# When the halo copy of sliding v and the loads behind it are issued, in an attention kernel overlapped with an MLP

## The chip, the cores and the metric

The kernel runs on one core of a Trainium2 chip. The metric is the device time of one execution, in microseconds (us). 13 runs of the kernel before took 307.81 to 313.6 us, with a median of 309.58 us.

A core has five engines with their own instruction queues: TensorE (PE: matmuls; PEld is its weight load), VectorE (DVE), ScalarE (ACT), GpSimd (POOL) and SyncE (SP). SP computes nothing here; it issues transfers. POOL issues transfers too, in another queue. Each engine executes its own instructions in order, so a wait at the head of a queue holds up all that stands behind it.

## The reference

What is computed, cut down (B, H, S, D = 8, 8, 576, 64; hidden width 2048):

```
scores = scale * q @ k.T                              # per batch row and head
mask_plain = (rel >= 0) & (rel < 32)                  # heads 0 to 3, "sliding"
mask_dil   = (rel >= 0) & (rel < 128) & (rel % 4 == 0)  # heads 4 to 7, "dilated"
attn = softmax(where(mask, scores, -1e9))
x    = (attn @ v).transpose(0, 2, 1, 3).reshape(4608, 512)
out  = relu(x @ w_in) ** 2 @ w_out                    # [512, 2048], [2048, 512]
```

rel is the position of the query less that of the key, so a query sees its last 32 positions, or each fourth of its last 128.

## The kernel before

**Attention.** The work goes by batch row b, 0 to 7. Sliding heads are cut into six blocks of 96 queries; a block's keys are its 96 positions and the 32 before them. So in `vp`, the fp16 tile of sliding v, partitions 32 to 127 hold a block's own values and partitions 0 to 31 the last 32 of the block before it. These 32 are the *halo*. `load_sliding_v` (L125) brings fp32 v into `sv`, `cast_sliding_v` (L167, three casts on POOL) makes `vp` of it, and the halo is copied inside `vp`: by `halo_sliding` (L182, ACT, in three parts) in rows 0 to 2, by `halo_sliding_by_dma` (L193, a transfer from SP) from row 3 on. Dilated v goes the same way: `load_dilated_v` (L134) to `sd`, `cast_dilated_v` (L173, four casts on POOL) to `vd`, and `halo_dilated` (L188) or `halo_dilated_by_dma` (L196).

Queries and keys must lie with the head dimension on partitions, in `QKTp` (sliding) and `QKTd` (dilated). From row 2 on the DMA transposes them. Sliding: POOL loads `ns` (L109), DVE reorders it by token into `nr` (L118), SP writes that to a DRAM tile `dp` (L214) and issues two transposes of it (`transpose_sliding`, L223), keys (i = 1) and then queries (i = 0). Dilated: POOL writes the DRAM tile `dd` (L204), SP issues two transposes of that (L227).

Per row, `attn_scores` (L692) makes the two sliding and two dilated groups of scores; each goes through exp on ACT and a mask multiplication on DVE (L564) into `AT`. The values follow: `av_sliding` (L616) for three pairs of blocks, `av_dilated` (L633) for the rest. Each is normalised on DVE (L605, L610) and turned into `xT`, the input of the MLP. Rows 1 to 3 do that on PE (`attn_values`, L706); rows 4 to 7 turn it by DMA (`attn_values_by_dma`, L737), with the tiles `xs`, `xd` and `yd`.

**The MLP as filler.** Tokens are worked in nine chunks of 512. `moe_gen` (L498) is a generator: 32 steps of the first product (L298; two full-width matmuls a step, relu on ACT L321, square on DVE L322), then the second product (L375, from chunk 2 on by one level of Strassen, with sums `gs` made on DVE at L331, L332 and L418). `pump(n)` takes n steps of it. The attention of row b is written between steps of chunk b - 1, so PE has matmuls while ACT and DVE work on scores; how many steps lie between two pieces of attention is a number in the code.

**The order of transfers** is the written one. While row b is worked, row b + 1 is made ready. In rows 2 and 3 one function does it, `turn_and_load` (L854): nr and dp, the load of sliding v, the load of dilated v, the sliding and the dilated transposes, all on SP, then both casts on POOL. Row 2 calls it after the third sliding product, row 3 after its last scores. From row 4 on it is three functions (L880 to L894): `copied` after the second sliding product, `first` and `second` after the transposes of yd. The halo transfers stand at the head of the next row (L851, L876), behind the stores of the MLP's results that were issued in between.

At the head of a row, POOL runs `after_transposes` (L234): it copies one element of `QKTd` into the tile `seen`, so that POOL waits there until the dilated query transpose has landed, and only then issues the loads of ns and dd for the next row. From row 5 on the cast of the row's dilated v stands behind these.

Two of the buffers of `ns` and `nr`, `QKTp`, `QKTd`, `vp` and `vd` exist, taken in turn; `sv` and `sd` exist once.

Of the kernel before, what the change touches and what calls it, by code (L numbers as in the profile page):

```python
# [17 lines left out]
def kernel(  # L18
# [9 lines left out]
    nc = tc.nc  # L28
# [105 lines left out]
    def load_dilated_v(b, eng):  # L134
        vv = v[b, HH:H].rearrange("h (i c) d -> i h (c d)", c=DIL)
        for t in range(2):
            eng.dma_start(out=sd[P - QD[t] : P, t, :, :], in_=vv[Q0D[t] : Q0D[t] + QD[t]])
# [29 lines left out]
    def cast_sliding_v(b, ms=range(0, NB, 2)):  # L167
        for m in ms:
            nc.gpsimd.tensor_copy(  # L169
                vp[b % 2][:, m : m + 2, :, 0:D], sv[:, :, m : m + 2, :].rearrange("p h m d -> p m h d")  # L170
            )

    def cast_dilated_v(b):  # L173
        for t in range(2):
            p0 = 64 * t
            for c in range(0, DIL, 2):
                nc.gpsimd.tensor_copy(  # L177
                    vd[b % 2][p0:P, t, c : c + 2, :, 0:D],
                    sd[p0:P, t, :, D * c : D * (c + 2)].rearrange("p h (c d) -> p c h d", d=D),
                )  # L180

    def halo_sliding(b, mp):  # L182
        m0, m1 = max(1, 2 * mp), 2 * mp + 2
        nc.scalar.copy(
            vp[b % 2][0:PADP, m0:m1, :, 0:D], vp[b % 2][P - PADP : P, m0 - 1 : m1 - 1, :, 0:D]
        )
# [6 lines left out]
    def halo_sliding_by_dma(b):  # L193
        nc.sync.dma_start(out=vp[b % 2][0:PADP, 1:NB], in_=vp[b % 2][P - PADP : P, 0 : NB - 1])
# [4 lines left out]
    def cast_v(b):  # L199
        cast_sliding_v(b)  # L200
        cast_dilated_v(b)
# [22 lines left out]
        for i in (1, 0):  # L224
            nc.sync.dma_start_transpose(out=QKTp[b % 2][:, i, :, PADP:], in_=dp[i])

    def transpose_dilated(b, dd):  # L227
        for i in (1, 0):
            nc.sync.dma_start_transpose(out=QKTd[b % 2][:, i, :, KPAD:], in_=dd[i])


# [280 lines left out]
    def pump(n):  # L512
        for _ in range(n):
            while pending:
                try:
                    next(pending[0])
                    break
                except StopIteration:
                    pending.pop(0)
# [46 lines left out]
    def s_sliding(b, hp):  # L566
        tiles = [pa(f"ps{b}_{hp}_{half}") for half in range(2)]
        for half, ps in enumerate(tiles):
            for m3 in range(3):
                m = 3 * half + m3  # L570
                for e in range(2):
                    r = slice(D * e, D * (e + 1))
                    nc.tensor.matmul(  # L573
                        ps[:, e, QB * m3 : QB * (m3 + 1)],
                        QKTp[b % 2][r, 1, hp, QB * m : QB * m + P],
                        QKTp[b % 2][r, 0, hp, PADP + QB * m : PADP + QB * (m + 1)],
                        start=True,
                        stop=True,
                    )
        for half, ps in enumerate(tiles):  # L580
            softmax(2 * hp + half, ps, maskp)
# [30 lines left out]
    def x_tiles(b):  # L612
        x = xp.tile([QB, 2, NB, 2, D], FP16, name=f"xs{b}", tag="xs")
        return x, [xp.tile([QD[t], DIL, HH, D], FP16, name=f"xd{b}_{t}", tag=f"xd{t}") for t in range(2)]
# [77 lines left out]
    def attn_scores(b, gap, less=0, hooks={}):  # L692
        for hp in range(2):
            s_sliding(b, hp)
            if hp in hooks:
                hooks[hp]()
            pump(gap)
        for g in range(2):
            s_dilated(b, g)
            if 2 + g in hooks:  # L700
                hooks[2 + g]()
            if g and b < 3:
                halo_sliding(b, 0)
            pump(gap - less)

    def attn_values(b, gap, wide=False, then=None):  # L706
        xs = x_tiles(b)
        for mp in range(3):
            av_sliding(b, mp, xs)
            if b < 3:  # L710
                if mp < 2:
                    halo_sliding(b, mp + 1)
                else:
                    halo_dilated(b, 0)
            if then and b == 2 and mp == 2:
                then()
            pump(gap)
        x_sliding(b, 0, xs, wide)
        if b < 3:
            halo_dilated(b, 2)  # L720
        pump(gap)
        av_dilated(b, 0, 0, xs)
        if then and b == 1:
            then()
        pump(gap)
        x_sliding(b, 1, xs, wide)
        pump(gap)
        av_dilated(b, 0, 1, xs)
        pump(gap)
        for a in range(2):  # L730
            av_dilated(b, 1, a, xs)
            pump(gap)
        x_dilated(b, 0, xs, wide)
        pump(gap)
        x_dilated(b, 1, xs, wide)
# [61 lines left out]
    dd = keep_dilated_qk(2)  # L797
# [28 lines left out]
    for a in range(2):  # L826
        t_dilated(1, m, a, True)
        pump(2)
    attn_scores(1, 2, 1)
    dp = []  # L830
    attn_values(1, 1, True, lambda: dp.append(keep_sliding_qk(2, by_token(2, ns))))
    pump(1000)
# [2 lines left out]
    leave_first()  # L835
    load_v(2)


    def turn(b, n):
        return keep_sliding_qk(b, by_token(b, n))  # L840

    for b in range(2, 4):
        pending.append(moe_gen(b - 1))
        nxt = b + 1
        after_transposes(b)
        ns = load_sliding_qk(nxt)
        if b == 2:
            cast_v(b)
        dd = keep_dilated_qk(nxt)
        if b == 3:  # L850
            halo_sliding_by_dma(b)  # L851
            halo_dilated_by_dma(b)

        def turn_and_load():  # L854
            dp = turn(nxt, ns)
            load_sliding_v(nxt)
            load_dilated_v(nxt, nc.sync)
            transpose_sliding(nxt, dp)
            transpose_dilated(nxt, dd)
            cast_v(nxt)  # L860

        pump(22 if b == 2 else 12)
        attn_scores(b, 4, 0, {3: turn_and_load} if b == 3 else {})
        attn_values(b, b, False, turn_and_load)
        pump(1000)

    for b in range(4, B):
        pending.append(moe_gen(b - 1))
        nxt = b + 1
        if nxt < B:  # L870
            after_transposes(b)
            ns = load_sliding_qk(nxt)
            dd = keep_dilated_qk(nxt)
        if b > 4:
            cast_dilated_v(b)
        halo_sliding_by_dma(b)  # L876
        halo_dilated_by_dma(b)
        dps = []

        def copied():  # L880
            if nxt < B:
                dps.append(turn(nxt, ns))

        def first(y):
            if nxt < B:
                load_sliding_v(nxt)

        def second(y):
            if nxt < B:
                transpose_sliding(nxt, dps[0])  # L890
                transpose_dilated(nxt, dd)
                load_dilated_v(nxt, nc.sync)
                nc.gpsimd.tensor_copy(seen, y[:, 0, 0, 0:1])
                cast_sliding_v(nxt)  # L894

        pump(3)
        attn_scores(b, 3)
        attn_values_by_dma(b, (copied, first, second))
        pump(1000)
# [33 lines left out]
```

## Time and profile before

| | |
|---|---|
| median of 13 runs | 309.58 us (307.81 to 313.6) |
| the profiled execution's own time | 311.42 us |
| its span, first to last instruction | 309.6 us |
| PE busy | 289.0 us, 93% of the span |
| DVE, ACT, POOL busy | 68%, 56%, 21% |
| the DMA queue of SP and ACT | 32.96 MB, 51.1% of 16 engines' span |
| the DMA queue of POOL | 13.63 MB, 25.8% |
| chain that ended last | PE 72%, DMA 12%, DVE 6%, SP's queue 4% |

How to read what follows. A *wait* line names the waiting engine, its line and what it waited for, then the sum in us, how often, and the longest. A *timeline* line has the start and the length in us, the engine, the line, the operation, out<-in with the tiles' names and their shapes, and how often in a row; square brackets hold the idle time before it and what ended it. The *chain of waits* is followed back from the last instruction, at each step to what released it. "Landing" is the time from a transfer's issue to the arrival of its data. The granted clock is TensorE's, as a share of full speed.

Times in the profile count from the span's start. Row 3's scores begin at about 100 us, row 4's at 127.9, row 5's at 157.6, row 6's at 190.4, row 7's at 224.3; from 254 us on only the MLP is left.

### The profile page before, as it was taken

Reading aid. Unit: us, or ns where it says so; the run is one execution under the profiler, and the core shown is the slowest. Engines: PE = TensorE matmul, PEld = TensorE weight load, DVE = VectorE, ACT = ScalarE, POOL = GpSimd, SP = SyncE. Lnnn points to the kernel's source line nnn. Section 1 sums busy time; section 2 is a strip of 40 time slices with the busy share of each in tenths; the row PEclk is TensorE's granted clock in tenths of the full one; section 3 lists DMA queues with packets and bytes.
Section 4 is the critical chain, followed back from the end, with each engine's and each line's share of the span. In section 5 each row is a group of like instructions: output and inputs, shape, how many; then the busy total and the mean of one; then the engine's idle time right before and its main releaser. Section 6 shows DMA issues by size and latency. Waiting matters only on the chain.

```text
span 309.6 us, 6899 instructions
## 1 busy us (share of the span) xinstructions
PE 289.0 (93%) x2762; PEld 193.5 (62%) x2762; DVE 210.8 (68%) x434; ACT 172.9 (56%) x293; POOL 64.7 (21%) x112
## 2 busy tenths in 40 slices
PE   1888998999999999999996999799999999999994
PEld 1555554455554579657886986358845885685584
DVE  7784449668844798499657975879389934834652
ACT  2856638569735942784475545554395436525620
POOL 4473008002806305300224003500240000000000
PEclk9999999999999999999999999989999999999999
DMA  7899997899599999987899789969993231003004
GB/s 116 166 216 213 208 169 135 200 196 224 109 230 190 233 211 161 257 160 138 155 185 261 156 132 199 274 125 140 145 270 26 42 93 62 2 1 135 2 1 139
DMA packets 77617, 47.04 MB, mean 152 GB/s; under 512 B 58480, under 2 KB 69232, under 8 KB 77584
## 3 DMA queue, kind: packets, MB, share of 16 engines
q1 hardware_dynamic: 68832, 32.96, 51.1%
q0 software_dynamic: 8752, 13.63, 25.8%
q8 instruction: 22, 0.36, 0.5%
q14 instruction: 11, 0.09, 0.1%
HBM read 36.70 MB, written 16.52 MB: 172 GB/s over the span
## 4 chain that ended last, share of the span: by engine, by line
PE 72%; DMA 12%; DVE 6%; SPq 4%; ACT 2%; issue 2%; POOL 1%; DVEq 0%; POOLq 0%
PE ph L298 32%; PE pa L375 16%; PE pb L375 7%; DMA vp<-vp 6%; PE po L441 5%; PE pc L375 4%; DVE AT L564 3%; DMA QKTd<-dd 3%; PE paw L638 2%; DMA QKTp<-dp 2%; PE pav L622 2%; DMA ns<-in_q_dram 1%; PE ps L573 1%; PE pf L507 1%; SPq L132 1%
## 5 line engine op out<-in xcount | busy, mean ns | idle before, releaser
L298 PE MATMUL ph<-xT,wi 128*128 128x512 f16 (+1 forms) x640 | 135.7, 361 | 0.7 <-ACT xT L675 0.7
L321 ACT ACTIVATE rt<-ph 128x512 f16<-128x512 f32 x144 | 86.2, 609 | 51.1 <-PE ph L298 49.6
L298 PEld LDWEIGHTS <-wi 128*128 128x128 f16 x640 | 68.4, 114 | 46.8 <-issue 2.0
L322 DVE TENSOR_TENSOR g<-rt 128x512 f16<-128x512 f16 x144 | 63.3, 448 | 40.7 <-ACT rt L321 39.2
L375 PEld LDWEIGHTS <-g 128*128 128x128 f16 x448 | 43.3, 98 | 6.1
L375 PEld LDWEIGHTS <-gs 128*128 128x128 f16 x336 | 32.2, 98 | 3.9 <-DVE gs L332 0.3
L441 PE MATMUL po<-wo,g 128*128 128x512 f16 x128 | 33.1, 379 | 0.0
L402 DVE TENSOR_TENSOR ov<-pb,ov 128x512 f32<-128x512 f32 x14 | 9.7, 692 | 31.1 <-PE pb L375 17.4
L375 PE MATMUL pa<-wt,gs 128*128 128x256 f16 x224 | 27.2, 273 | 0.0
L375 PE MATMUL pb<-wt,g 128*128 128x256 f16 x224 | 27.1, 273 | 0.0
L169 POOL CAST vp<-sv 128x512 f16<-128x512 f32 x24 | 14.8, 648 | 54.2 <-DMA sv<-in_v_dram 47.5
L391 ACT COPY ov<-pa 128x512 f32<-128x512 f32 x14 | 8.2, 586 | 30.7 <-PE pa L375 30.7
L177 POOL CAST vd<-sd 128x512 f16<-128x512 f32 (+1 forms) x32 | 22.6, 732 | 11.6 <-DMA sd<-in_v_dram 11.2
L610 DVE TENSOR_TENSOR xd<-paw,rcp_d 80x512 f16<-80x512 f32 (+1 forms) x32 | 21.9, 684 | 1.1
L563 ACT ACTIVATE AT<-pz 128x576 f16<-128x576 f32 x32 | 19.7, 694 | 1.2 <-PE pz L592 1.1
L564 DVE TENSOR_TENSOR AT<-AT,maskd 128x576 f16<-128x576 f16 x32 | 18.9, 617 | 1.9 <-ACT AT L563 0.8
L563 ACT ACTIVATE AT<-ps 128x576 f16<-128x576 f32 x32 | 19.2, 657 | 1.3 <-PE ps L573 0.8
L564 DVE TENSOR_TENSOR AT<-AT,maskp 128x576 f16<-128x576 f16 x32 | 16.2, 520 | 5.2 <-ACT AT L563 3.5
L622 PEld LDWEIGHTS <-AT 128*128 128x128 f16 x192 | 9.5, 99 | 13.7 <-issue 9.8
L391 ACT COPY ou<-pa 128x512 f32<-128x512 f32 x14 | 8.2, 586 | 17.4 <-PE pa L375 17.4
L622 PE MATMUL pav<-vp,AT 128*128 128x65 f16 x192 | 10.9, 196 | 7.4 <-DMA vp<-vp 5.7
L610 DVE TENSOR_TENSOR xs<-pav,rcp_p 96x512 f16<-96x512 f32 x24 | 16.5, 687 | 0.8
(80 smaller groups left out, 278.3 us busy)
## 6 DMA issues: line engine op xcount, KB each, us to landing
sv<-in_v_dram SPq DMA_DIRECT2D x14, 288.0 KB, 5.3
dp<-nr SPq DMA_DIRECT2D x12, 288.0 KB, 4.2
out_dram<-ou SPq DMA_DIRECT2D x6, 512.0 KB, 4.1
out_dram<-ov SPq DMA_DIRECT2D x6, 512.0 KB, 4.6
sd<-in_v_dram SPq DMA_DIRECT2D x8, 320.0 KB, 6.1
ns<-in_k_dram POOLq DMA_DIRECT2D x8, 288.0 KB, 6.3
ns<-in_q_dram POOLq DMA_DIRECT2D x8, 288.0 KB, 7.7
sd<-in_v_dram SPq DMA_DIRECT2D x8, 256.0 KB, 6.2
```

The lines of the kernel that those rows point to most:

```text
L169: nc.gpsimd.tensor_copy(vp[b % 2][:, m : m + 2, :, 0:D], sv[:, :, m : m + 2, :].rearrange("p h m d -> p m h d"))
L177: nc.gpsimd.tensor_copy(vd[b % 2][p0:P, t, c : c + 2, :, 0:D], sd[p0:P, t, :, D * c : D * (c + 2)].rearrange("p h (c d) -> p c h d", d=D),)
L298: nc.tensor.matmul(ph[:, t0:t1], wi4[ffc // 4][:, dmk, :, ffc % 4], xT[:, dmk, x0 : x0 + t1 - t0], start=(dmk == 0 and t0 == 0), stop=(dmk ...
L321: nc.scalar.activation(rt, ph[:], ACTF.Relu)
L322: nc.vector.tensor_mul(g[:, ffc, :], rt, rt)
L375: nc.tensor.matmul(banks[bank][:, t], a(k, t), b(k), start=(new and t == 0 and k == 0), stop=(k == HF - 1), skip_group_check=True,)
L391: nc.scalar.copy(ot, banks[A])
L441: nc.tensor.matmul(po, g[:, ffc, t * P : (t + 1) * P], wo[ffc // 4][:, ffc % 4, :], start=(ffc == 0), stop=(ffc == NFF - 1),)
L563: nc.scalar.activation(AT[:, u, 0:UW], ps[:, :, 0 : UW // 2], ACTF.Exp, scale=scale)
L564: nc.vector.tensor_mul(AT[:, u, 0:UW], AT[:, u, 0:UW], mask)
L610: nc.vector.tensor_tensor(out=x, in0=pv, in1=rb, op=ALU.mult)
L622: nc.tensor.matmul(pav[:, i, h * (D + 2) : h * (D + 2) + D + 1], AT[:, 2 * (h // 2) + m // 3, off : off + P], vp[b % 2][:, m, h, 0 : D + 1 ...
```

## The change

1. `transpose_dilated` takes the sides that it is to do. A new function does four things in a row: the dilated keys' transpose, the halo transfer of sliding v, the dilated queries' transpose, the load of dilated v. So for rows 3 to 7 the halo's issue leaves the head of the row and stands between the two transposes on SP. It reads what POOL's sliding cast writes, so SP waits there for that cast.
2. In `turn_and_load` (making ready rows 3 and 4) the load of dilated v goes behind all four transposes. The sliding cast stays; the dilated cast goes to the head of the row, on POOL behind `seen` and the loads of ns and dd, where rows 5 to 7 already had it.
3. From row 4 on, the sliding cast is written before the dilated transposes. POOL's own order is the same.
4. Row 2 calls `turn_and_load` after its second sliding product, not its third.
5. Row 3's scores begin after 9 steps of the MLP, not 12.
6. Row 1's first halo copy (ACT) stands after its second group of sliding scores, not after its last dilated scores.

```diff
-    def transpose_dilated(b, dd):
-        for i in (1, 0):
+    def transpose_dilated(b, dd, sides=(1, 0)):
+        for i in sides:
             nc.sync.dma_start_transpose(out=QKTd[b % 2][:, i, :, KPAD:], in_=dd[i])
...
-            if g and b < 3:
+            if g and b == 2:
                 halo_sliding(b, 0)
...
-            if then and b == 2 and mp == 2:
+            if then and b == 2 and mp == 1:
                 then()
...
-    attn_scores(1, 2, 1)
+    attn_scores(1, 2, 1, {1: lambda: halo_sliding(1, 0)})
...
+    def transpose_and_load(b, dd):
+        transpose_dilated(b, dd, (1,))
+        halo_sliding_by_dma(b)
+        transpose_dilated(b, dd, (0,))
+        load_dilated_v(b, nc.sync)
...
         if b == 3:
-            halo_sliding_by_dma(b)
+            cast_dilated_v(b)
             halo_dilated_by_dma(b)
 
         def turn_and_load():
             dp = turn(nxt, ns)
             load_sliding_v(nxt)
-            load_dilated_v(nxt, nc.sync)
             transpose_sliding(nxt, dp)
-            transpose_dilated(nxt, dd)
-            cast_v(nxt)
-
-        pump(22 if b == 2 else 12)
+            cast_sliding_v(nxt)
+            transpose_and_load(nxt, dd)
+
+        pump(22 if b == 2 else 9)
...
-        if b > 4:
-            cast_dilated_v(b)
-        halo_sliding_by_dma(b)
+        cast_dilated_v(b)
         halo_dilated_by_dma(b)
...
         def second(y):
             if nxt < B:
                 transpose_sliding(nxt, dps[0])
-                transpose_dilated(nxt, dd)
-                load_dilated_v(nxt, nc.sync)
                 nc.gpsimd.tensor_copy(seen, y[:, 0, 0, 0:1])
                 cast_sliding_v(nxt)
+                transpose_and_load(nxt, dd)
```

## The prediction

> **What bounds the kernel now.** The first view is the page: PE is busy 93% of the span and its chain is 72% PE, so a saving must be a place where PE waits. The waits of PE name one that this change touches: 5.7 us in three places, for the copy of the sliding v halo (vp<-vp).
>
> ```profile
> PE pav L622 <- DMA vp<-vp: 5.7, 3, 2.7
> ```
>
> Next, busy time by stretch, one stretch from the first scores of a row to the next row's: rows 3, 4, 5, 6, 7. Behind each length stand PE, PEld, DVE, ACT, POOL busy, then PE's clock.
>
> ```profile
> 99.80:127.60 27.80, 27.31 (x299) 19.72 (x298) 21.79 (x44) 15.40 (x28) 6.87 (x13) 1.00 1.12 206
> 127.60:157.40 29.80, 29.80 (x295) 21.34 (x294) 23.03 (x48) 18.03 (x31) 4.46 (x9) 1.00 0.89 169
> 157.40:190.20 32.80, 30.09 (x349) 27.01 (x347) 24.67 (x48) 17.92 (x31) 7.74 (x13) 1.00 0.95 185
> 190.20:224.10 33.90, 31.59 (x290) 21.31 (x288) 24.44 (x48) 17.93 (x31) 7.49 (x13) 0.95 0.91 176
> 224.10:253.70 29.60, 28.94 (x285) 20.36 (x284) 22.79 (x46) 17.88 (x30) 3.14 (x4) 1.00 0.48 100
> ```
>
> Row 4 has no idle PE and takes 29.8 us. Rows 5 and 6 do the same work in 3.0 and 4.1 us more. The chain shows why in row 5: the second dilated transpose lands, GpSimd's one-element read sees it, and only then is the halo issued, behind the v loads and two stores; it needs 7.1 us.
>
> ```profile
> 154.67 0.75 SPq L229
> ...
> 155.51 4.59 DMA QKTd<-dd
> ...
> 160.22 0.35 POOL seen L235
> 160.58 7.11 DMA vp<-vp
> ...
> 167.73 0.29 PE pav L622 x4
> ```
>
> The timeline has the stop in each row, and the DVE copy nr<-ns, which turns the next row's q and k and runs next but one behind it on DVE:
>
> ```profile
> 138.44 0.75 DVE L120 COPY nr<-ns 128x2304 f16<-128x2304 f16 x1
> ...
> 167.73 0.29 PE L622 MATMUL pav<-vp,AT 128*128 128x65 f16 x4 [2.71 <-DMA vp<-vp]
> ...
> 171.17 0.75 DVE L120 COPY nr<-ns 128x2304 f16<-128x2304 f16 x1
> ...
> 200.06 0.33 PE L622 MATMUL pav<-vp,AT 128*128 128x65 f16 x4 [2.31 <-DMA vp<-vp]
> ...
> 200.20 2.75 PE L298 MATMUL ph<-xT,wi 128*128 128x512 f16 x6
> ...
> 204.80 0.74 DVE L120 COPY nr<-ns 128x2304 f16<-128x2304 f16 x1
> ...
> 232.30 0.29 PE L622 MATMUL pav<-vp,AT 128*128 128x65 f16 x4 [0.66 <-DMA vp<-vp]
> ```
>
> In row 6 six matmuls take 2.75 us where row 7 has 1.46: after the 2.31 us stop the granted clock was 0.52 from 200.06 to 203.6, which costs about 1.7 us more. Row 5's 2.71 us stop was not followed by that. [...]
>
> **The halo, rows 5 to 7.** It goes between the two dilated transposes, at 155.5 in row 5. It must wait for GpSimd's sliding cast, which in the old rows ends at 154.44, 187.12 and 220.95, while the first dilated transpose leaves SP at 155.4, 188.5 and 221.7: no wait. It needs 2.8 to 7.5 us to land (the extremes of its five issues), so by 163.0 at the latest in row 5, and PE asks at 165.0. The three stops go.
>
> What is late next? The halo's issue (0.61 to 1.10 us on SP) stands before the second transpose, so that, the dilated v load, both stores, and GpSimd's "seen" read come later. Bounds: 0.2 us, if the transpose queue is what limits SP here (one transpose took 2.39 us to issue in row 5, 1.27 in row 6), to 1.1. I take 0.7, nearest to the 0.61 and 0.68 issues among the quieter queues. Behind "seen" on GpSimd stand the loads of ns and dd and the cast of the dilated v, and ns feeds nr. The landings from issue, rows 5 and 6:
>
> ```profile
> DMA to landing us min/median/max: 7.3/7.7/8.2
> DMA to landing us min/median/max: 8.7/9.1/9.5
> ```
>
> The later ns half is issued at 161.44 and 193.31, so it lands at 169.6 and 202.8. New: +0.7, and -0.3 because 82.5 KB of halo (at the 270 GB/s of the page's fullest slices) no longer lie in front: 170.0 and 203.2. Row 4 shows what an unhindered row wants: nr 3.56 us after the first pav (134.88 to 138.44), that is 168.3 and 201.0. So DVE will wait where PE waited. From nr on, DVE has no gap for 7.8 us in rows 4, 5 and 6 (138.44 to gs L332 at 146.25; 171.17 to 178.99; 204.80 to 212.70), and PE's product from gs starts within 0.7 us of that. The vd halo, 0.7 later as well, lands at about 171.7 in row 5; its reader comes 9.5 us after the first pav (row 4), at 174.2: covered. The row therefore ends earlier by what nr gains: 171.17 - 170.0 = 1.2 in row 5, 204.80 - 203.2 = 1.6 in row 6 (the slow clock's 1.7 us goes, but ns hides most of it). Bounds: 0 (ns 1.6 us later than I say) to 2.9 and 3.8 (nr at 168.3 and 201.0).
>
> Row 7 has no nr, but DVE is busy until 233.2 with masks and squares, and the normalisation starts there: of 0.66 us I take 0.3 (0 to 0.66).
>
> **Rows 3 and 4.** Row 3's turn moves one sliding product earlier: nr at about 82.5 instead of 83.83. The 0.74 us copy now delays the third normalisation; its next reader on PE is over 1 us later: nothing. SP then issues dp and sv, and no longer sd (2.74 us of issue, 89.28 to 92.0) before the sliding transposes. They landed at 100.05, and PE waited 0.2 us for them; new about 97. The pump of 12 becomes 9, so scores begin three steps of 0.435 us earlier, 98.5 instead of 99.8: covered by 1.5 us; no matmul is added or dropped. Gain 0.2. The halo now waits on SP for the cast (sv lands about 93.8, three casts of 0.62: 95.8), and behind it are the second dilated transpose (landing about 100.3, wanted at 102.9), sd, three stores and the vd halo (wanted after 115). In row 4 it waits alike, to about 120.7, and the transpose lands near 125, wanted at 131. Each is covered.
>
> The dilated cast is what pays. It ran at 97.1 to 100.1 and 121.6 to 124.0, ahead of the scores. New: it follows "seen" and four load issues (0.56 to 0.66 us each) and waits for sd; I put it at 104.5 to 107.5 and 128.2 to 131.3, beside the scores. There DVE slows:
>
> ```profile
> L564 DVE TENSOR_TENSOR AT<-AT,maskp x4: 457/458/459, 128.9 to 131.5; 128x576 f16<-128x576 f16 x4
> L564 DVE TENSOR_TENSOR AT<-AT,maskd x4: 459/778/862, 162.3 to 165.8; 128x576 f16<-128x576 f16 x4
> ```
>
> The first four masks (row 4, no cast beside them) take 0.46 us, those beside row 5's cast (163.15 to 166.31) mostly 0.78. In 3.1 us of cast DVE does 3.1 / 1.7 = 1.8 us of work and falls 1.3 behind; row 4 has 0.4 to 0.5 us of DVE gaps there, so nr moves by 0.8 and PE's product, with 0.2 of slack, by 0.6 (0 to 0.8). [...]
>
> Row 3 has that, and its ns load: "seen" about 100.4, ns issued by 102.3, landing 5.9 later as now (8.2 if it meets sd as in row 5), 108.2 to 110.5; nr is wanted at about 107.3, as three pumps put two 0.69 us sums behind it. One more normalisation (0.9 us) also comes before PE's product. Against it, nr itself is no later than the old 109.99. Between 0 and 1.7 us lost I take 0.5, since row 3 has the widest gaps (2.2 us a step for 1.85 of DVE work).
>
> **Row 1.** Its first halo copy (0.40 us, ACT) moves before the dilated scores and removes PE's 0.54 us wait at 51.76. PE then waits longer at 53.80 for a normalisation that stands behind eight masks on DVE: 0 (from -0.5 to +0.2).
>
> **Sum:** -1.2 -1.6 -0.3 -0.2 +0.6 +0.5 +0 = -2.2 us. The profiled execution took 311.42 us (span 309.6 and 1.8 around it), so 309.2 there; it lies 1.84 above the median of the runs, 309.58. Against the median: 307.4 us.
>
> **Rivals.** Full gain: ns lands in time because the stores move behind it. Then only DVE's own lag stands: its work before the normalisation ended at 166.95 and 199.35, nr could start 2.48 later (row 4: 135.96 to 138.44), 169.4 and 201.9: -1.8 -2.9 -0.3 -0.2 = -5.2, 304.4 us. For it: row 4's ns landed in 6.9 us. Against it: sd, which row 4 had loaded earlier, stays in the way in rows 5 and 6.
>
> Slower: the second dilated transpose comes 2 us late instead of 0.7, because a plain copy between two transposes drains the queue; no row of before has one there. Rows 3, 5 and 6 lose 1.3 each through ns and nr: -2.2 + 3.9 = +1.7, 311.3 us. It is slower than before from 0.7 + 2.2 / 3 = 1.4 us of delay on. Against it: yd's transposes are followed by sv's copies 0.05 us later.
>
> No change: the halo, in a queue behind three transposes, lands as late for PE as before, or what PE gains in rows 5 and 6 is given back in 3 and 4: 309.6 us.
>
> **How the numbers follow.** Forecast 0.45 (own range 306 to 309.5), full gain 0.18, slower 0.25, no change 0.12. Half a per cent, 1.55 us, is about what a measurement of this kernel tells from no change. Faster: 0.36 + 0.18 = 0.54; same: 0.09 + 0.10 + 0.03 = 0.22; slower: 0.22 + 0.02 = 0.24. The range 304.2 to 311.7 leaves out about half of the full-gain case below (its far end, nr at 168.3 and 201.0, is -2.9 -3.8 -0.3 -0.2 = -7.2, 302.4) and a tenth above (rows 3 and 4 at their worst, +2.5, with nothing gained in 5 and 6, are +2.0, 311.6).
>
> **What would show it.** Right: no PE wait for vp<-vp in rows 5 to 7; idle DVE before nr<-ns there, ended by ns; no stretch at half clock in row 6; casts of vd beside the masks of rows 3 and 4 and rows 4 to 6 all near 30.5 to 32 us. Wrong: nr without a wait (more gain), "seen" over 1.4 us later relative to the first dilated transpose (less), or a wait of PE for QKTp or QKTd in row 3.

## The result and the profile after

The changed kernel takes 311.78 us, the median of 11 runs (310.55 to 313.78). The kernel before, run beside it, took 309.39 us (median of 48 runs). The ratio is 1.0072, 95% interval 1.0042 to 1.0101: **slower by 0.7%**, where 307.4 us was forecast. The profiled execution took 311.58 us, with a span of 309.7. The ratios here and below leave out slow executions (over 1.5% above the fastest of their kernel) and lie up to 0.35% from the quotients of the medians, which are over all of them.

The waits of PE in the kernel after. A line names the waiting engine and line and what it waited for, then the sum in us, how often, and the longest:

```profile
PE pav L622 <- DVE xs L610: 3.6, 1, 3.6
...
PE pa L375 <- DVE gs L332: 1.0, 2, 0.5
```

The wait for vp<-vp is gone, all 5.7 us of it. One stop of 3.6 us has come: a sliding product waits for a normalisation on DVE.

Busy time by stretch of the kernel after: first the rows 3 to 7 as before (start and end in us, length, then PE, PEld, DVE, ACT, POOL busy, PE's clock, share and rate of the DMA), then four stretches of 3.41 us around the stop:

```profile
99.10:132.60 33.50, 29.91 (x305) 20.98 (x305) 23.90 (x45) 16.53 (x30) 12.46 (x21) 0.95 1.03 200
132.60:162.40 29.80, 29.80 (x297) 21.38 (x296) 23.03 (x48) 18.04 (x31) 1.85 (x4) 1.00 0.78 153
162.40:193.80 31.40, 30.50 (x347) 26.53 (x346) 24.48 (x48) 17.94 (x31) 7.54 (x13) 1.00 0.97 191
193.80:225.10 31.30, 30.36 (x289) 20.46 (x288) 24.21 (x48) 17.91 (x31) 7.50 (x13) 1.00 0.94 191
225.10:254.20 29.10, 29.10 (x287) 20.55 (x287) 23.07 (x47) 17.72 (x30) 3.00 (x4) 1.00 0.53 107
...
107.26:110.67 3.41, 3.41 (x31) 2.02 (x30) 1.67 (x4) 1.70 (x4) 0.31 (x1) 1.00 1.17 194
110.67:114.08 3.41, 0.46 (x3) 0.00 (x0) 3.12 (x7) 1.08 (x2) 0.00 (x0) 1.00 1.07 219
114.08:117.49 3.41, 2.77 (x18) 1.78 (x19) 3.34 (x9) 0.60 (x1) 0.00 (x0) 0.50 1.02 229
117.49:120.91 3.42, 3.42 (x45) 3.13 (x44) 3.32 (x6) 1.23 (x2) 1.45 (x2) 1.00 1.26 208
```

The last number but two is the clock. Row 3 takes 33.5 us instead of 27.8. Part of that only moved: with 9 steps instead of 12, row 3's scores begin three steps earlier and row 2 is 1.6 us shorter. Rows 2 and 3 together take 60.7 us (27.2 from 71.9 to 99.1, and 33.5) where the kernel before took 56.5 (28.77 + 27.76): **4.2 us lost**. Rows 5 and 6 are 1.4 and 2.6 us shorter than in the first profile of before.

The chain of waits of the kernel after, around the stop (start, length, what):

```profile
101.94 0.19 POOL seen L235
...
102.46 0.65 POOL ns L112
103.11 7.73 DMA ns<-in_q_dram
...
110.86 0.76 DVE nr L120
111.62 0.68 DVE g L322 x2
...
112.32 0.70 DVE gs L331
...
113.05 0.69 DVE gs L332
113.74 0.12 DVE rcp_p L605
...
113.89 0.70 DVE xs L610
...
114.72 0.59 PE pav L622 x8
```

So the path runs from POOL's `seen` over the load of ns, which takes 7.7 us, to nr, and then through all that is written behind nr on DVE. Only the last two of these pieces on DVE free the PSUM buffer (the tile `pav`, where PE's products stand until they are normalised) that PE waits for. The same work in the kernel before, DVE's and PE's timeline:

```profile
107.92 0.69 DVE L331 TENSOR_TENSOR gs<-g 128x1024 f16<-128x1024 f16 x1
...
108.65 0.69 DVE L332 TENSOR_TENSOR gs<-gs,g 128x1024 f16<-128x1024 f16 x1
...
109.99 0.76 DVE L120 COPY nr<-ns 128x2304 f16<-128x2304 f16 x1
...
111.57 0.69 DVE L610 TENSOR_TENSOR xs<-pav,rcp_p 96x512 f16<-96x512 f32 x1
...
112.40 0.41 PE L622 MATMUL pav<-vp,AT 128*128 128x65 f16 x8 [0.28 <-DVE xs L610]
```

There the two gs sums stood ahead of nr, ns landed just in time, and PE's stop was 0.28 us. The second half of ns was issued at 104.12 there and took 5.9 us; in the kernel after it is issued earlier, at 103.11, and takes 7.7 us.

Rows 5 and 6 are limited by ns as forecast. DVE's timeline of the kernel after, the rows' nr, with the idle time before it in brackets:

```profile
104.55 2.55 DVE L564 TENSOR_TENSOR AT<-AT,maskd 128x576 f16<-128x576 f16 x2 [0.27 <-ACT AT L563]
...
110.86 0.76 DVE L120 COPY nr<-ns 128x2304 f16<-128x2304 f16 x1 [1.93 <-DMA ns<-in_q_dram]
...
174.71 0.76 DVE L120 COPY nr<-ns 128x2304 f16<-128x2304 f16 x1 [0.67 <-DMA ns<-in_q_dram]
...
206.01 0.76 DVE L120 COPY nr<-ns 128x2304 f16<-128x2304 f16 x1 [0.74 <-DMA vd<-vd]
```

(In row 6 ns landed at 205.93, so ns holds that nr too, though the bracket names vd.) The first line is for later: two masks beside the cast of dilated v took 2.55 us.

### The profile page after: what moved, and what is told of

The parts are those of the page before. It is cut to its first block, busy times and chain, and to the rows that moved or that the text cites. A ratio compares the mean times of both kernels' runs of the same rounds, so it can differ in the third digit from the quotient of the medians.

```text
span 309.7 us, 6888 instructions
## 1 busy us (share of the span) xinstructions
PE 290.4 (94%) x2762; PEld 192.6 (62%) x2762; DVE 209.6 (68%) x434; ACT 172.9 (56%) x293; POOL 64.1 (21%) x112
## 4 chain that ended last, share of the span: by engine, by line
PE 67%; DMA 12%; DVE 11%; issue 3%; ACT 3%; POOL 2%; SPq 1%; POOLq 0%; DVEq 0%
PE ph L298 29%; PE pa L375 15%; PE pb L375 8%; DMA ns<-in_q_dram 5%; PE po L441 5%; DMA sv<-in_v_dram 4%; PE pc L375 3%; DVE g L322 2%; DMA vd<-vd 2%; PE paw L638 2%; DVE xd L610 2%; ACT AT L563 1%; DVE xs L610 1%; PE pav L622 1%; PE ps L573 1%
## 5 line engine op out<-in xcount | busy, mean ns | idle before, releaser
L322 DVE TENSOR_TENSOR g<-rt 128x512 f16<-128x512 f16 x144 | 62.0, 443 | 38.7 <-ACT rt L321 37.5
L375 PEld LDWEIGHTS <-g 128*128 128x128 f16 x448 | 43.7, 99 | 7.5 <-DVE g L322 0.6
L402 DVE TENSOR_TENSOR ov<-pb,ov 128x512 f32<-128x512 f32 x14 | 9.7, 692 | 31.1 <-PE pb L375 18.0
L169 POOL CAST vp<-sv 128x512 f16<-128x512 f32 x24 | 15.6, 681 | 50.8 <-DMA sv<-in_v_dram 50.8
L391 ACT COPY ov<-pa 128x512 f32<-128x512 f32 x14 | 8.2, 586 | 31.5 <-PE pa L375 31.5
L177 POOL CAST vd<-sd 128x512 f16<-128x512 f32 (+1 forms) x32 | 22.6, 735 | 12.7 <-DMA sd<-in_v_dram 10.4
L638 PEld LDWEIGHTS <-AT 128*128 128x128 f16 x256 | 11.7, 98 | 7.0 <-PE ph L298 1.5
L441 PEld LDWEIGHTS <-g 128*128 128x128 f16 x128 | 10.4, 97 | 8.3
L622 PEld LDWEIGHTS <-AT 128*128 128x128 f16 x192 | 9.1, 99 | 10.0 <-issue 5.2
```

The lines of the kernel that those rows point to most:

```text
L169: nc.gpsimd.tensor_copy(vp[b % 2][:, m : m + 2, :, 0:D], sv[:, :, m : m + 2, :].rearrange("p h m d -> p m h d"))
L177: nc.gpsimd.tensor_copy(vd[b % 2][p0:P, t, c : c + 2, :, 0:D], sd[p0:P, t, :, D * c : D * (c + 2)].rearrange("p h (c d) -> p c h d", d=D),)
L322: nc.vector.tensor_mul(g[:, ffc, :], rt, rt)
L375: nc.tensor.matmul(banks[bank][:, t], a(k, t), b(k), start=(new and t == 0 and k == 0), stop=(k == HF - 1), skip_group_check=True,)
L441: nc.tensor.matmul(po, g[:, ffc, t * P : (t + 1) * P], wo[ffc // 4][:, ffc % 4, :], start=(ffc == 0), stop=(ffc == NFF - 1),)
L622: nc.tensor.matmul(pav[:, i, h * (D + 2) : h * (D + 2) + D + 1], AT[:, 2 * (h // 2) + m // 3, off : off + P], vp[b % 2][:, m, h, 0 : D + 1 ...
```

## The experiments

Two theories of the lost 4.2 us. **Theory A**: nr in row 3 waits for ns. With 9 steps DVE wants ns earlier, and ns lands later, because its load takes longer. nr stands on DVE ahead of the first normalisation, so PE stops. **Theory B**: the cast of dilated v, now beside row 3's masks, slows DVE, and PE waits for that. A third question is whether rows 5 and 6 gained at all. All runs were compared with the kernel before on the same chip (309.06 to 309.40 us there). The row lengths below are differences of the starts of each row's first sliding scores. Stops are idle times of PE.

**The kernel after with 12 steps again**, twice:

```diff
-        pump(22 if b == 2 else 9)
+        pump(22 if b == 2 else 12)
```

> Edit: the changed kernel with row 3's scores after 12 steps of the MLP again, not 9. Theory A (the copy waits): in row 3 of the changed kernel DVE stands 1.93 us at nr<-ns until ns lands at 110.84, everything behind it on DVE (two squares, two sums, the first normalisation) comes late, and PE stands 3.59 us before its third sliding product. Three steps more are 1.3 us, and the two 0.69 us sums then stand ahead of the copy again, so it is wanted about 2.7 us later: DVE's wait falls to at most 0.9 us, PE's stop to 0.3 to 1.2, the stretch at half clock in row 3 goes. Time 311.8 - 3.5 = about 308 us. Theory B (the cast): the loss is the cast of the dilated v beside row 3's masks, which 12 steps leave beside the masks; PE's stop stays over 2.5 us and the time stays at 311.8 within 0.7.

> No new edit: the changed kernel with 12 steps a second time, beside the others, for the size of its gain. Theory A: 2 to 2.5 us under the kernel before (306.9 against 309.3 in its first timing); PE's stop in row 3 under 1.2 us; rows 5 and 6 still wait for ns. If the first timing was luck, it is within 0.8 us of the kernel before.

Measured: 306.9 us (10 runs), ratio 0.9955 [0.9915, 0.9995], and on another chip 308.08 us (12 runs), 0.9937 [0.9901, 0.9973]. Rows 2 and 3 take 56.8 and 56.9 us. DVE's and PE's timeline of the first of them:

```profile
108.16 0.69 DVE L331 TENSOR_TENSOR gs<-g 128x1024 f16<-128x1024 f16 x1
...
108.88 0.69 DVE L332 TENSOR_TENSOR gs<-gs,g 128x1024 f16<-128x1024 f16 x1
...
110.33 0.76 DVE L120 COPY nr<-ns 128x2304 f16<-128x2304 f16 x1
...
112.74 0.41 PE L622 MATMUL pav<-vp,AT 128*128 128x65 f16 x8 [0.86 <-DVE xs L610]
```

ns landed at 110.31 here, only half a microsecond earlier than in the kernel after. But the two gs sums are done before nr instead of behind it, PE asks later, and the stop is 0.86 us instead of 3.59. There is no half clock in row 3 (the mean clock of that execution is 1.0). The casts stay beside the masks (104.21 to 107.14). So the edit from 12 to 9 steps costs what is lost, and theory B is left with at most the 0.3 to 0.5 us that rows 2 and 3 still lose. Everything else in the change together gains 0.45 to 0.63%. Where, the two profiles don't show in full (the first is of an execution of 309.36 us, 2.5 above its median): row 7 and what follows is 0.8 to 1.3 us shorter than before, but rows 5 and 6 together take 65.0 and 63.1 us, where two profiles of the kernel before have 66.7 and 62.6.

**The kernel before with 9 steps alone:**

```diff
-        pump(22 if b == 2 else 12)
+        pump(22 if b == 2 else 9)
```

> Edit: the kernel before with row 3's scores after 9 steps of the MLP, not 12; nothing else. Theory A: ns lands at 110.0 as before, but the copy nr<-ns is wanted about 2.7 us earlier, at 107.3; DVE waits 1.5 to 2.7 us there, PE stops about 3 us before its third sliding product, and half clock may follow (1.7). Time 309.4 + 3 to 4.5 = 312.4 to 314 us. Theory B: the cast of the dilated v stays ahead of the scores here, so nothing is lost: 309.4 within 0.7 us.

Measured: 316.67 us (4 runs, 313.36 to 318.61), ratio 1.0274 [1.0188, 1.036]. Two of the four took 318.6 us, and the profiled one, 313.36, is the shortest: slower, but by how much is not settled, and in the profile not mainly where theory A puts it. PE's and SP's timeline:

```profile
108.57 0.76 DVE L120 COPY nr<-ns 128x2304 f16<-128x2304 f16 x1 [0.70 <-DMA ns<-in_q_dram]
...
112.44 0.41 PE L622 MATMUL pav<-vp,AT 128*128 128x65 f16 x8 [1.21 <-DVE xs L610]
...
128.66 0.41 SPq L397 DMA_DIRECT2D out_dram<-ov  x1
...
129.16 0.61 SPq L194 DMA_DIRECT2D vp<-vp  x1
...
139.36 0.29 PE L622 MATMUL pav<-vp,AT 128*128 128x65 f16 x4 [2.91 <-DMA vp<-vp]
```

In row 3 the stop behind nr is 1.21 us, with 0.65 us more before the scores, for QKTp. The largest loss is in row 4: its halo is issued at the head of the row behind the stores, at 129.16, lands at 139.32, and PE waits 2.91 us. So without the rest of the change the 9 steps cost mainly through this late halo, and with it they still cost more than they save. The 3.6 us stop needs both: 9 steps, and the later ns of the changed order. In row 3 here ns was issued at 103.30 and took 5.2 us; in the kernel after it was issued at 103.11 and landed 2.3 us later. So not `seen` made it late but the load itself. What the changed order puts just ahead of that load is sd (issued from 99.87 instead of from about 89); that sd is the cause is not shown, as no run moves it alone.

**The kernel after, row 3's nr behind the first normalisations** (the turn is called after the second sliding product, no longer from the scores):

```diff
-            if then and b == 2 and mp == 1:
+            if then and b in (2, 3) and mp == 1:
...
-        attn_scores(b, 4, 0, {3: turn_and_load} if b == 3 else {})
+        attn_scores(b, 4)
```

> Edit: the changed kernel, still with 9 steps, but row 3 calls its turn (copy nr<-ns, transfers and casts for row 4) after its second sliding product, as row 2 does, and not after its last scores. Theory A: the first two normalisations now stand ahead of the copy on DVE, so that PE's products find their buffers free; PE's stop in row 3 falls from 3.59 to under 0.7 us, and the transfers for row 4 come 2 to 3 us later but are covered, since row 4's sliding transposes landed over 10 us before its scores. Time 311.8 - 3.5 = about 308 us. Theory B: the cast for row 3 is where it was; the time stays at 311.8 within 0.7.

Measured: 308.07 us (10 runs), ratio 0.9992 [0.9959, 1.0025]. Rows 2 and 3 take 57.3 us. DVE's and PE's timeline:

```profile
110.15 0.69 DVE L610 TENSOR_TENSOR xs<-pav,rcp_p 96x512 f16<-96x512 f32 x1
...
110.98 0.41 PE L622 MATMUL pav<-vp,AT 128*128 128x65 f16 x8 [0.74 <-DVE xs L610]
...
112.26 0.75 DVE L120 COPY nr<-ns 128x2304 f16<-128x2304 f16 x1
```

9 steps, the same casts and the same load, and the stop is 0.74 us: what costs is that nr, with its wait, stands ahead of the normalisation. That is the second half of theory A.

**The kernel after, ns released by the keys' transpose** (`seen` reads the first dilated transpose's tile, no longer the second's):

```diff
-        nc.gpsimd.tensor_copy(seen, QKTd[b % 2][:, 0, 1, KPAD : KPAD + 1])
+        nc.gpsimd.tensor_copy(seen, QKTd[b % 2][:, 1, 1, KPAD : KPAD + 1])
```

> Edit: the changed kernel, but GpSimd's one-element read before the loads of ns and dd looks at the dilated keys' transpose (the first) and not the queries' (the second). Theory A: ns is issued and lands earlier by the distance of the two landings (2.6 us in row 3, 1.3 and 1.5 in rows 5 and 6 of the changed kernel): row 3's DVE wait of 1.93 and PE's stop of 3.59 go to under 0.7, and rows 5 and 6 gain up to 1.3 each. Time 311.6 - 4 = 307.5 us. Theory B (cast beside the masks): the casts of dilated v come up to 1 us earlier but stay beside the masks; the time stays at 311.5 within 0.7. Against A: loads that start sooner share the queues with the second transpose and the dilated v and may land hardly earlier; then 310.5.

Measured: 308.8 us (12 runs), ratio 0.9996 [0.9963, 1.0029]. ns is issued 2.2 us earlier (100.88 instead of 103.11) and lands 1.6 us earlier, at 109.21. The stop in row 3 falls from 3.59 to 1.66 us, and the half clock behind it is gone (the mean clock of the profiled execution is 1.0, where it is 0.987 in the kernel after). In row 2 a new stop of 0.90 us comes, for POOL's sliding cast.

**Both, 12 steps and the earlier release:**

```diff
-        nc.gpsimd.tensor_copy(seen, QKTd[b % 2][:, 0, 1, KPAD : KPAD + 1])
+        nc.gpsimd.tensor_copy(seen, QKTd[b % 2][:, 1, 1, KPAD : KPAD + 1])
...
-        pump(22 if b == 2 else 9)
+        pump(22 if b == 2 else 12)
```

> Edit: both together: the changed kernel with row 3's scores after 12 steps, and the one-element read on the keys' transpose. Theory A: row 3 as with 12 steps alone (its stop of 0.86 us gone too), and in rows 5 and 6, where DVE waited for ns at nr and PE stopped 1.0 and 1.9 us behind it with 12 steps alone, ns lands 1.2 to 1.5 us earlier, so these stops fall under 0.5. Time 306.9 - 1.5 = 305.4 us. If the loads are only slowed by starting sooner: 306.9 within 0.7.

Measured: 308.4 us (12 runs), ratio 0.9991 [0.9958, 1.0024]: no better than 12 steps alone. The stop in row 3 is 1.09 us and the one in row 2 1.12 us. In row 6 ns is issued at 194.13 and needs 10.4 us. Counted from the row's first scores it is issued 2.0 to 2.4 us earlier than in the two profiles with 12 steps alone and lands 1.0 to 1.4 us earlier: much of the earlier issue goes into a longer transfer. The profiled execution, 310.33 us, is the longest of the twelve.

**The kernel after, ns loaded a whole turn earlier**, in rows 2 and 3 behind the sliding cast, from row 4 on behind nr, so that 13 to 32 us lie between its issue and its nr, where rows 3, 5 and 6 of the kernel after have 8 to 9:

```diff
-        ns = load_sliding_qk(nxt)
+        if b == 2:
+            nss = {3: load_sliding_qk(3)}
...
-            dp = turn(nxt, ns)
+            dp = turn(nxt, nss[nxt])
...
             cast_sliding_v(nxt)
+            nss[nxt + 1] = load_sliding_qk(nxt + 1)
             transpose_and_load(nxt, dd)
...
-            ns = load_sliding_qk(nxt)
...
-                dps.append(turn(nxt, ns))
+                dps.append(turn(nxt, nss[nxt]))
+                if nxt + 1 < B:
+                    nss[nxt + 1] = load_sliding_qk(nxt + 1)
```

> Edit: the changed kernel, still with 9 steps, but the load of ns for the row after next is issued earlier on GpSimd: in rows 2 and 3 behind the sliding cast, ahead of the one-element read; from row 4 on right behind the turn. So ns lies ready long before nr. Theory A (the copy waits for its load): row 3's stop of 3.6 us falls under 0.5 and its half clock goes; rows 5 and 6 (31.1 to 31.5 us) come to 29.8 to 30.5. Time 311.5 - 3.3 - 1.7 - 2 = 304.5 us. Theory B (the dilated cast beside the masks): row 3 keeps a stop of over 1.5 us and takes over 30 us with 9 steps whatever ns does; time over 308. Against A: the earlier load takes DMA time from the transposes and v loads, and PE stops for these instead.

Measured: 308.28 us (12 runs), ratio 0.9955 [0.9918, 0.9992]. No nr waits for ns any more. The waits of PE:

```profile
PE pz L592 <- DMA QKTd<-dd: 4.0, 2, 2.2
...
PE pav L622 <- DVE rcp_p L605: 1.3, 1, 1.3
```

The next thing is late: the dilated transposes, in rows 3 (1.81 us) and 6 (2.15 us). In row 3 the early ns is issued beside them: the second transpose, at 97.54, stands next to ns at 97.44 and lands after 7.6 us, where it takes 3.4 in the kernel after. In row 6 no ns is loaded at that time (the last was issued at 174), and why the transpose takes 6.2 us there is open. Both stops were followed by half clock, 0.50 from 106.20 and from 198.36 us. The profiled execution, 311.47 us, is the longest of the twelve.

**Early ns and 12 steps**, the edit above and this one:

```diff
-        pump(22 if b == 2 else 9)
+        pump(22 if b == 2 else 12)
```

> Edit: as the run before it (ns loaded early), but row 3's scores after 12 steps. Theory A: the number of steps cost time only through the wait for ns, so this takes what 9 steps take with the early load, within 1 us: 304.7. If 9 steps cost something by themselves (later stores, later scores of row 4), this one is 1.5 us or more faster than the one with 9.

Measured: 306.63 us (6 runs, 305.91 to 307.01), ratio 0.9900 [0.9854, 0.9945], the shortest of all and faster than both kernels. The waits of PE:

```profile
PE pz L592 <- DMA QKTd<-dd: 1.2, 1, 1.2
PE pav L622 <- DVE xs L610: 1.1, 1, 1.1
```

With 12 steps the scores come later, and of the 4.0 us at QKTd 1.2 remain. Rows 2 and 3 together still take about 2 us more than in the kernel before, but rows 5 and 6, with no wait for ns, take 30.6 and 30.3 us. On that chip 12 steps without the early ns had 0.9937 [0.9901, 0.9973]; the intervals overlap, so how much the early ns adds is not settled.

**The kernel before with the earlier halo in rows 5 to 7 alone:**

```diff
-    def transpose_dilated(b, dd):
-        for i in (1, 0):
+    def transpose_dilated(b, dd, sides=(1, 0)):
+        for i in sides:
...
-        halo_sliding_by_dma(b)
+        if b == 4:
+            halo_sliding_by_dma(b)
...
-                transpose_dilated(nxt, dd)
-                load_dilated_v(nxt, nc.sync)
                 nc.gpsimd.tensor_copy(seen, y[:, 0, 0, 0:1])
                 cast_sliding_v(nxt)
+                transpose_dilated(nxt, dd, (1,))
+                halo_sliding_by_dma(nxt)
+                transpose_dilated(nxt, dd, (0,))
+                load_dilated_v(nxt, nc.sync)
```

> Edit: the kernel before with the halo transfer between the two dilated transposes in rows 5 to 7 alone; rows 1 to 4, the steps and the dilated casts are as before. Theory A: the three stops of PE for the halo go, rows 5, 6 and 7 gain what they gained in the changed kernel (1.3, 0.9 to 2.6 by whether the kernel before met half clock in row 6, and 0.3 to 0.8), and nothing is lost in row 3. Time 309.4 - 3 = 306.4 us (305.5 to 307.5). Rival C: the halo between two transposes costs the rest of the row what PE gains, because the second transpose, the stores and the loads behind it come later; 309.4 within 0.7.

Measured: 308.93 us (10 runs), ratio 0.9976 [0.9936, 1.0016]: no gain that can be told from none. The halo stops are gone in the profile, and rows 5 and 6 take 31.5 and 31.2 us, much as in the kernel after. So the row lengths forecast for after (31.6 and 32.3 us) are about right, and what was wrong is what they were compared with. The next two runs settle that.

**The kernel before and the kernel after once more**, without an edit:

> No edit: the kernel before, profiled a second time, since its first profile (311.42 us) lay 2 us above its median and the halo change alone gave only 0.3 us of the 3 expected. If the stops are a fixed part of this kernel, PE again waits 5 to 6 us for vp<-vp in rows 5 to 7, and the gain that was missing is lost elsewhere. If the first profile was an unlucky execution, the three waits come to 3 us or less, ns lands about as late, and the change had less to win than the first profile showed. Time 309.3 either way.

> No edit: the changed kernel, profiled a second time on the same chip as the others. Theory A: DVE again waits 1 to 2 us at row 3's nr<-ns and PE stops 2.5 to 4 us before its third sliding product; row 3 (from its first scores to row 4's) takes 31 us or more. Time 311.5 us. If that stop was an accident of the first profile, row 3 takes under 29 us and the time near 311.5 needs another cause.

Measured: 309.13 us (12 runs, ratio 1.0004 [0.9977, 1.0031]) and 311.45 us (11 runs, ratio 1.0073 [1.0039, 1.0107]). The waits of PE in the second profile of before (span 306.2 us):

```profile
PE pav L622 <- DMA vp<-vp: 3.6, 3, 1.5
```

The three halo stops are 1.09, 1.46 and 1.10 us here, where they were 2.71, 2.31 and 0.66. Its busy time by stretch, rows 5 and 6:

```profile
157.80:189.00 31.20, 30.11 (x349) 26.99 (x348) 24.45 (x48) 17.93 (x31) 7.28 (x13) 1.00 0.98 196
189.00:220.40 31.40, 29.94 (x291) 20.82 (x290) 24.54 (x48) 17.92 (x31) 7.15 (x13) 1.00 0.96 188
```

Rows 5 and 6 take 31.2 and 31.4 us, just what they take in the two profiles of after (31.5 and 31.3; 31.1 and 31.5). ns had landed at 168.67 and 200.47 and nr followed 1.07 and 0.74 us later: even without the halo stop, nr could move by no more than that.

The second profile of after shows the same stop, 3.60 us. Summed by rows, from the second profile of before to that of after: up to row 2 +0.1, rows 2 and 3 +4.4, row 4 +0.3, rows 5 and 6 0.0, row 7 and the rest -1.3: +3.5 us, the difference of the spans (306.2 and 309.7). The medians differ by 2.3 us, since that execution of before (308.06 us) lies 1.1 under its median.

**The kernel before with row 1's halo copy earlier:**

```diff
-            if g and b < 3:
+            if g and b == 2:
...
-    attn_scores(1, 2, 1)
+    attn_scores(1, 2, 1, {1: lambda: halo_sliding(1, 0)})
```

> Edit: the kernel before with row 1's first halo copy moved ahead of the dilated scores; nothing else. Prediction's reading: PE's 0.54 us wait at the first sliding product of row 1 goes, but the next wait for the normalisation behind DVE's masks grows by as much: 309.1 us, within 0.4 of the kernel before. If the shorter row 1 of the changed kernel's first profile (24.4 against 25.4 us) was made by the move, 308.1 us.

Measured: 309.62 us (12 runs), ratio 1.0013 [0.9974, 1.0052]. PE's 0.54 us wait for the copy goes, and its next wait, for the reciprocal, grows from 0.64 to 1.14 us.

## Why the prediction was wrong, point by point

The medians put against the before of the same chip:

| kernel | us | ratio | rows 2 + 3, us | stop of PE before the third sliding product, row 3, us |
|---|---|---|---|---|
| before | 309.39 | | 56.5, 56.3 | 0.28, 0.28 |
| after, 9 steps | 311.78; 311.45 | 1.0072; 1.0073 | 60.7; 60.8 | 3.59; 3.60 |
| after, 12 steps | 306.9; 308.08 | 0.9955; 0.9937 | 56.8; 56.9 | 0.86; 0.89 |
| after, nr behind the normalisations | 308.07 | 0.9992 | 57.3 | 0.74 |
| after, ns released earlier | 308.8 | 0.9996 | 58.9 | 1.66 |
| after, early ns, 12 steps | 306.63 | 0.9900 | 58.3 | 1.07 |

**The step that failed is row 3's +0.5**, with its bounds 0 to 1.7: "Between 0 and 1.7 us lost I take 0.5, since row 3 has the widest gaps". It measured +4.2 to +4.4. Its first half was about right: ns was to land between 108.2 and 110.5 and be wanted at about 107.3; it landed at 110.84, 0.3 us past the bound, and DVE, which came to it at 108.93, waited 1.9 us. Two estimates on the way were short: sv landed at 95.72, not 93.8, so the halo was issued at 97.81, not 95.8, and `seen` came at 101.92, not 100.4. The load then took 7.7 us, between the 5.9 and 8.2 that were named. What was wrong above all is what the lateness costs.

- "nr itself is no later than the old 109.99" was used as a relief. It came at 110.86, and the old nr was just in time for a PE that came 1.3 us later, with the two gs sums (0.69 us each) already done. With 9 steps PE asks earlier by the 1.3 us and finds the sums behind nr. So the first normalisation, which stood 1.58 us behind nr (109.99 to 111.57), now stands 3.03 us behind it (110.86 to 113.89). The prediction named the sums and the early scores, and did not add them on PE's side.
- The gaps of DVE could not take it up, because DVE was idle in front of the work, not behind it: 1.93 us of waiting, then nr and six instructions without a gap. PE has two PSUM buffers for these products and stops at the third.
- The stop was followed by half clock. From 114.08 to 117.49 PE was busy for 2.77 us at 0.50, by estimate half of that, 1.4 us, of lost work. That was not priced at all for row 3.

Together: 3.59 - 0.28 for the stop, 1.4 for the clock, less the 0.2 at QKTp, is 4.5 us, against 4.2 measured. With 12 steps rows 2 and 3 lose 0.3 to 0.5 us, near the 0.5 that was taken.

**The base of rows 5 and 6.** The forecast row lengths follow from 32.8 - 1.2 = 31.6 and 33.9 - 1.6 = 32.3; measured 31.1 to 31.5 in both. The mechanism, ns instead of the halo, is right: DVE idles before nr, ended by ns. But the profiled execution of before, 1.84 us above its median, had these 1.2 and 1.6 us, and more, as its own excess (its rows 5 and 6 are 1.6 and 2.5 us longer than in the second profile): halo stops of 5.7 us in sum where another execution has 3.6, and a stretch at half clock (0.50 from 200.16 to 203.57). Subtracting its whole saving from the median counted that excess twice. By the second profile of before, rows 5 and 6 gain 0; the halo edit alone measured -0.2% [-0.6, +0.2].

**The other steps.**
- The halo stops in rows 5 to 7: gone, right. Row 7 and what follows gained 0.8 to 1.3 us, where 0.3 was taken with 0.66 at most. The second profile has 1.10 us of stop there.
- The second dilated transpose later by 0.2 to 1.1 us: right. From the end of the first dilated transpose's issue to `seen` it is 5.2 us in row 5 and 4.2 to 4.3 in row 6 of the two profiles of the kernel after, where those of the kernel before have 4.7 to 4.8 and 3.5 to 3.6: 0.4 to 0.9 us more. ns landed 12.3 and 12.1 us after the rows' starts, where 12.6 and 13.0 follow from the forecast.
- Row 3's wait for QKTp (-0.2): gone, right.
- The cast beside the masks in row 4 (+0.6): 0. Row 4 takes 29.8 us as before (30.1 in the second profile, with 0.28 us of waiting for row 5's QKTp at its end). In the kernel after the cast ends at 132.33, before the scores; with 12 steps it does lie beside the masks (two of them take 0.86 us), and row 4 still takes 29.8. In row 3 the cast slowed masks as said, but DVE waits for ns just behind them, which hides it.
- Row 1: nothing, right, and the wait behind it grew as said.
- The rival "slower" named 311.3 us, near the measured time, but by another way: a second transpose 2 us late, and losses in rows 3, 5 and 6. The transpose was not that late (0.4 to 0.9 us, above), no run shows the drained queue that it supposed, and the measured loss is in row 3 alone.

The whole change without its edit to 9 steps, at 0.9955 and 0.9937, lies about where -2.2 us would put it (0.993). That is luck as far as the profiles tell: rows 5 and 6 don't give the 2.8 us of the sum there, and row 7 and the rest give more than its 0.3.

**Open.** Why 9 steps still cost about 1.6 us more than 12 when ns is early (308.28 against 306.63): the profile shows later dilated transposes for earlier scores, but it is the longest of those runs. Why the load of ns in row 3 takes 2 us longer in the changed order. Where the rest of the gain of 12 steps lies. And why the halo stops of one kernel vary from 3.6 to 5.7 us between executions.

## What to carry to other kernels

When scores or products are moved earlier, every wait in front of them grows by that much: write down for each instruction that may wait what stands behind it on its in-order engine, and how many buffers the consumer has left, since a wait of 1.9 us can become a stop of 3.6. Before saving a stop that a profile shows, find what would be late next (here ns, about 1 us behind) and see in a second execution whether the stop is always that long; the saving belongs to the execution in which it was seen. A part that only gives the consumer work earlier (12 steps to 9) is to be tried by itself: it turned a gain of half a per cent into a loss.

## What the runs showed of the hardware

**Half clock behind stops of PE.** In the first profiles of the kernel before and the kernel after and in that of early ns, each stretch at clock 0.50 away from the end of the run lasted 3.41 us. The kernel after has them from 25.33 and from 114.08 us, 88.75 us apart, which is 26 times 3.413; early ns has them from 106.20 and 198.36, 92.16 us apart, 27 times 3.413. Counted in such lengths from the one at 200.16, the first profile of the kernel before has these stretches (PE busy is the first number behind the length):

```profile
162.61:166.02 3.41, 2.41 (x37) 2.05 (x35) 3.33 (x6) 2.77 (x6) 3.35 (x6) 1.00 1.10 336
166.02:169.44 3.42, 1.71 (x25) 1.70 (x25) 2.14 (x5) 0.67 (x2) 0.29 (x1) 1.00 1.14 190
169.44:172.85 3.41, 3.41 (x48) 3.39 (x45) 2.90 (x8) 2.07 (x4) 0.00 (x0) 1.00 0.78 157
196.74:200.16 3.42, 1.11 (x13) 0.62 (x11) 2.61 (x6) 1.43 (x3) 1.26 (x2) 1.00 1.18 236
200.16:203.57 3.41, 3.41 (x19) 1.52 (x18) 1.32 (x3) 1.18 (x2) 0.00 (x0) 0.50 1.05 211
```

The prediction could only note that row 5's stop of 2.71 us kept the clock and row 6's of 2.31 us did not. Counted so, row 5's lies in two stretches, with 1.00 and 1.71 us of idle PE, and row 6's in a single one. Stretches of the profiles here, by their idle PE:

| profile | stretch, us | PE idle in it, us | clock in the next |
|---|---|---|---|
| kernel after | 110.67 to 114.08 | 2.95 | 0.50 |
| kernel before, first | 196.74 to 200.16 | 2.31 | 0.50 |
| early ns | 194.95 to 198.36 | 2.15 | 0.50 |
| kernel before with 9 steps | 137.35 to 140.76 | 2.01 | 1.00 |
| kernel after with 12 steps, first | 202.91 to 206.32 | 1.86 | 1.00 |
| early ns | 102.79 to 106.20 | 1.82 | 0.50 |
| kernel before, first | 166.02 to 169.44 | 1.71 | 1.00 |
| kernel after | 21.92 to 25.33 | 1.31 | 0.50 |

(The fourth and fifth are of executions without half clock in their middle and are counted from the one at their end, which is less sure. In the last, PE also makes the transposes of the first rows.) So the idle time in such a stretch does not settle it alone: 1.31 and 1.82 us were followed by half clock, 1.86 and 2.01 us were not. That in row 5 and row 6 it was the place of the stop which decided is the author's reading; no run moves a stop to test it.

The stop of 3.59 us in the first profile of the kernel after was followed by half clock, 0.50 from 114.08; in the second, with a stop of 3.60 us, the mean clock over row 3 is 0.95 as in the first. The mean clock of the executions fits that: one such stretch takes by estimate 3.41 x 0.50 = 1.7 of some 310 us, or about 0.0055, off it, and it was 0.994 or less in 20 of 23 executions of the kernel after, in 2 of 22 with 12 steps, and in 17 of 88 of the kernel before beside them.

**Masks beside a cast.** A mask multiplication takes 0.46 us alone. Of the 21 that overlap one of POOL's casts in the kernel after, eleven took 0.83 to 0.87 us and one 1.76 us (two of them are the line of DVE's timeline above), the others 0.46 to 0.71. So most lost 0.4 us, less than a whole cast (0.61 us). The prediction took an even slowdown by 1.7, which is 0.78 us a mask; none of the 21 took that, and no run tests what makes these times. What it cost could not be seen in any row.

**The load of ns, issued earlier.** With the earlier release the query half of ns was issued 2.2 us earlier in row 3 and landed 1.6 us earlier. It took 5.9 us in row 3 of the first profile of before and 5.2 in the kernel before with 9 steps, both in that kernel's order; in the changed order it took 7.7 us in the kernel after, 7.8 in the first profile with 12 steps (102.50 to 110.31) and 8.3 with the earlier release (100.88 to 109.21). In row 6 with 12 steps and the earlier release it took 10.4.
